# Softmax sums in attention: the 1e-9 added on VectorE, without GpSimd's two small additions

## The chip, the cores and the metric

The kernel runs on one core of a Trainium2 chip. The metric is device time in microseconds (us) of one execution. PE is TensorE, PEld its weight loads, DVE VectorE, ACT ScalarE, POOL GpSimd and SP the engine that issues the DMAs.

## The reference, cut to what matters

Block-causal attention over 8 batches of 8 heads (576 positions, 64 wide, blocks of 64), then a feed-forward layer whose activation is a rational function.

```python
scores = scale * np.matmul(q, k.transpose(0, 1, 3, 2))
scores = np.where(mask, scores, -1000000000.0)
scores = scores - np.max(scores, axis=-1, keepdims=True)
attn = np.exp(scores)
attn = attn / (np.sum(attn, axis=-1, keepdims=True) + 1e-09)
attn_out = np.matmul(attn, v)
# x: attn_out as 4608 tokens of 512
h = x @ w_in                                   # 2048 wide
P = a[0] + a[1] * h + a[2] * h**2 + a[3] * h**3
Q = 1.0 + np.abs(b[0]) * np.abs(h) + np.abs(b[1]) * h**2
out = (P / (Q + 1e-6)) @ w_out
```

## The kernel before, in words

**Attention** works on 32 visits, each a pair of heads of one batch. A visit has five query tiles t = 0 to 4 of 64, 128, 128, 128 and 128 rows, with 64, 192, 320, 448 and 576 keys, and both heads j = 0, 1 of a tile: ten items per visit, 320 in all. `load` fetches q, k and v on SP's queue; `prep` transposes q and k on PE and splits each into a high and a low part; three DMAs place the parts into kq. For each item `scores` multiplies into PSUM (L432, L433, mask in L436), and DVE takes the negative row maximum into nm (L437). For t = 4 the row of 576 keys lies in two PSUM banks, so there are two maxima, joined in L440.

One item later `expo` runs. ACT takes the exponential (L449) into the tile pt and writes each row's sum to sm: sm[:, j, 0], and for t = 4 a second part in sm[:, j, 1]. After the second head of a tile the group of both heads is normalised. For t = 4 POOL adds the two parts of sm (L455). POOL adds 1e-9 into the small tile rc (L456), DVE takes its reciprocal in place (L457), and POOL multiplies the probabilities by it: the first 64 keys into pk (L458), the rest in place (L462, once per head, t > 0 only). That is one group per query tile: 160 groups, 32 of them with t = 4. Nine items after the group's second head, `transp` transposes the probabilities on PE (L481) and splits them (ACT L486, DVE L487), and `pv` multiplies them by v (L500). The tiles rc, nm and sm have four buffers each; a pt of each size has one, and pk has two.

**The feed-forward layer** runs in two phases over the hidden width. The first takes 1280 of the 2048 hidden columns, in units that are emitted between the attention steps as soon as a batch's tokens are there; the second follows attention. A unit is a first product on PE (L207), the rational function on ACT, POOL and DVE (L214 to L219, L224 to L232), a split of g into gh on ACT (L239) and gl on POOL (L240), and the second product on PE (L257), which needs gl and gh.

**The weights** come as float64 bit patterns and are taken apart into two float32 parts by `place` (L129 to L149, on ACT, POOL and DVE). Of its 32 steps four are emitted by step 36 of attention, sixteen from step 44 to 59 and twelve from step 80 to 230.

**The order of work** on each engine is set when the program is built: the loops emit in the order of `attn_steps` and `Ffn.steps`, and the framework then settles the order of the instructions of each engine and places the waits. Each engine works its own list strictly in order.

The lines that matter here are L437, L440, L449, L455 to L462, L481, L240 and L257.

Of the kernel before, what the change touches and what calls it, by code (L numbers as in the profile page):

```python
# [14 lines left out]
ALU = mybir.AluOpType  # L15
# [46 lines left out]
def attn_ffn_kernel(  # L62
# [11 lines left out]
    nc = tc.nc  # L74
# [234 lines left out]
    with ExitStack() as actx:  # L309
# [101 lines left out]
        def pieces(t):  # L411
            return [(0, NK[t])] if t < 4 else [(0, 288), (288, 288)]
# [30 lines left out]
        def expo(p, t, j):  # L443
            s = st_[p]
            nq, n = NQ[t], NK[t]
            pt, pk, nm, sm = s[t]
            banks = s.pop((t, j))
            for i, (c0, w) in enumerate(pieces(t)):
                nc.scalar.activation(out=pt[:nq, j, c0:c0 + w], in_=banks[i][:nq, :w], func=AF.Exp,  # L449
                                     bias=nm[:nq, j, 0:1], scale=1.0, accum_out=sm[:nq, j, i:i + 1])  # L450
            if j == 0:
                return
            rc = att.tile([128, 2], F32, name=f"rc{p}_{t}", tag="rc", bufs=4)
            if t == 4:
                nc.gpsimd.tensor_tensor(out=sm[:, :, 0], in0=sm[:, :, 0], in1=sm[:, :, 1], op=ALU.add)  # L455
            nc.gpsimd.tensor_scalar_add(rc[:nq], sm[:nq, :, 0], 1e-9)  # L456
            nc.vector.reciprocal(rc[:nq], rc[:nq])  # L457
            nc.gpsimd.tensor_tensor(out=pk[:nq], in0=pt[:nq, :, 0:64],  # L458
                                    in1=rc[:nq].unsqueeze(2).to_broadcast([nq, 2, 64]), op=ALU.mult)
            if t > 0:  # L460
                for jj in range(2):
                    nc.gpsimd.tensor_scalar(out=pt[:nq, jj, 64:n], in0=pt[:nq, jj, 64:n],  # L462
                                            scalar1=rc[:nq, jj:jj + 1], scalar2=1.0,
                                            op0=ALU.mult, op1=ALU.mult)
# [48 lines left out]
        def attn_steps():  # L513
# [8 lines left out]
            for k in range(len(items) + ALAG2 + ALAG3 + 8):  # L522
                for x in [x for x in todo if x[0] == k]:
                    todo.remove(x)
                    x[1](*x[2])
                if k < len(items):
                    p, t, j = items[k]
                    ts = visits[p][1]
                    if (t, j) == (ts[0], 0):
                        if p + 1 < NV:  # L530
                            o0, o1, o2 = OFFS[len(ts)]
                            at(k + o0, load, p + 1)
                            at(k + o1, prep, p + 1, 0)
                            at(k + o2, prep, p + 1, 1)
                    at(k + ALAG2, expo, p, t, j)
                    if j == 1:
                        lag = min(ALAG3, nxt[k] - 1)
                        at(k + lag, transp, p, t)
                        if t in (2, 4):
                            at(k + lag + 1, pv, p, t // 4)  # L540
                            if t == ts[-1] and p + 1 < NV:
                                at(k + lag + 1, vprep, p + 1)
                    scores(p, t, j)
                yield k
# [87 lines left out]
```

## Time and profile before

| | |
|---|---|
| median of 3 runs | 1382.86 us (1381.88 to 1384.8) |
| the profiled execution | 1380.84 us |
| its span, first to last instruction | 1379.1 us |
| busy share: PE, PEld, DVE, ACT, POOL | 93%, 83%, 74%, 66%, 69% |
| instructions: DVE, POOL | 2048, 1240 |
| mean granted TensorE clock | 0.974 of full speed |

The busy share is an average over the span. The span has stretches of different kinds: attention starts up while weights are taken apart (to about 175 us), attention and the first phase of the feed-forward layer run side by side (to about 970 us), then the second phase runs alone.

### The profile page before, as it was taken

The page shows a single profiled execution, that of the slowest core. Times are in us where ns is not written, and L with a number is a line of the kernel's source. Part 1 is how long each engine was busy: PE and PEld are TensorE (multiplying, and loading weights), DVE is VectorE, ACT ScalarE, POOL GpSimd, SP SyncE. Part 2 cuts the span into 40 slices and gives each one's busy share as a digit, 9 for nine tenths or more (in the row PEclk, how much of TensorE's full clock was granted, in tenths as well). Part 3 has the DMA queues.
Part 4 walks back from the last instruction along what each step waited for, and adds up shares of the span by engine and source line. Part 5 has one row for each costly group of instructions (what it writes and reads, how often), then busy time and mean ns, then how long its engine had stood idle before and what let it go on. Part 6 is the DMA issues. An engine that isn't in the chain of part 4 may idle for free.

```text
span 1379.1 us, 24416 instructions
## 1 busy us (share of the span) xinstructions
PE 1278.1 (93%) x8088; PEld 1149.6 (83%) x8088; DVE 1027.2 (74%) x2048; ACT 909.4 (66%) x2250; POOL 958.2 (69%) x1240
## 2 busy tenths in 40 slices
PE   4677899999899979999999999999989999999997
PEld 3667788999888879888998999998979888888885
DVE  5898877787778857887767777776676767676675
ACT  4766767777677756777767777776645655555553
POOL 4889987687678747777767676666556666666654
PEclk9788999999999999999999999999999999999999
DMA  9778556666556655665654555652632233333332
GB/s 216 198 196 238 146 150 166 168 166 181 148 145 150 164 151 132 165 166 153 157 140 123 154 134 122 160 127 65 213 141 77 77 123 123 122 123 123 122 113 86
DMA packets 216925, 200.84 MB, mean 146 GB/s; under 512 B 129504, under 2 KB 184800, under 8 KB 216800
## 3 DMA queue, kind: packets, MB, share of 16 engines
q1 hardware_dynamic: 216736, 199.28, 53.6%
q8 instruction: 65, 1.06, 0.3%
q14 instruction: 60, 0.49, 0.1%
q0 software_dynamic: 64, 0.00, 0.0%
HBM read 98.57 MB, written 44.04 MB: 103 GB/s over the span
## 4 chain that ended last, share of the span: by engine, by line
PE 69%; DVE 9%; POOL 9%; DMA 5%; ACT 3%; issue 3%; SPq 1%; POOLq 0%; DVEq 0%; ACTq 0%
PE h L207 25%; PE o L257 24%; PE o L500 8%; PE t L481 4%; PE s L432 3%; PE s L433 2%; PE tp L366 2%; POOL gl L240 1%; POOL p L462 1%; DMA x<-xscr 1%; POOL u L217 1%; DVE v L231 1%; DVE nm L437 1%; POOL v L216 1%; DMA xscr<-x 1%
## 5 line engine op out<-in xcount | busy, mean ns | idle before, releaser
L207 PE MATMUL h<-x,wih 128*128 128x256 f32 (+1 forms) x1872 | 415.7, 313 | 9.0 <-DMA x<-xscr 7.9
L207 PEld LDWEIGHTS h<-x,wih 128*128 128x128 f32 x1872 | 309.7, 191 | 29.1 <-issue 6.6
L207 PE MATMUL h<-x,wil 128*128 128x256 f32 (+1 forms) x936 | 290.7, 311 | 0.0
L240 POOL TENSOR_TENSOR gl<-s,gh 128x512 fp32r<-128x512 f32 x144 | 188.8, 1313 | 106.4 <-ACT gh L239 103.0
L257 PE MATMUL o<-woh,gl 128*128 128x512 f32 x576 | 232.2, 403 | 12.1 <-POOL gl L240 10.6
L257 PE MATMUL o<-wol,gh 128*128 128x512 f32 x576 | 227.7, 396 | 0.0
L257 PE MATMUL o<-woh,gh 128*128 128x512 f32 x576 | 227.7, 395 | 0.0
L437 DVE TENSOR_REDUCE nm<-s 128x1 f32<-128x288 f32 (+4 forms) x384 | 161.7, 427 | 78.4 <-PE s L436 45.2
L449 ACT ACTIVATE p<-s,nm 128x288 f32<-128x288 f32 (+4 forms) x384 | 184.9, 485 | 48.3 <-DVE nm L437 35.0
L217 POOL TENSOR_TENSOR u<-v,u 128x512 f32<-128x512 f32 x144 | 189.6, 1317 | 9.8
L216 POOL TENSOR_SCALAR v<-u,bab 128x512 f32<-128x512 f32 x144 | 118.9, 826 | 98.1 <-ACT u L214 94.6
L207 PEld LDWEIGHTS h<-x,wil 128*128 128x128 f32 x936 | 178.7, 191 | 8.7
L462 POOL TENSOR_SCALAR p<-p,rc 128x128 f32<-128x128 f32 (+3 forms) x256 | 164.8, 655 | 29.6 <-DVE rc L457 27.7
L218 DVE TENSOR_TENSOR s<-s,h 128x512 f32<-128x512 f32 x144 | 98.5, 684 | 100.1 <-ACT s L215 99.4
L432 PE MATMUL s<-kq 128*128 128x256 f32 (+3 forms) x384 | 137.3, 360 | 24.3 <-DMA kq<-hl 8.9
L224 ACT ACTIVATE v<-u,qcb 128x512 f32<-128x512 f32 x144 | 104.6, 726 | 69.6 <-POOL u L217 68.9
L214 ACT ACTIVATE u<-h 128x512 f32<-128x512 f32 x144 | 85.9, 596 | 94.2 <-PE h L207 90.1
L239 ACT CAST gh<-s 128x512 fp32r<-128x512 f32 x144 | 89.2, 623 | 82.1 <-DVE s L232 81.5
L257 PEld LDWEIGHTS o<-woh,gl 128*128 128x128 f32 x576 | 109.2, 190 | 35.5 <-POOL gl L240 14.3
L257 PEld LDWEIGHTS o<-wol,gh 128*128 128x128 f32 x576 | 109.1, 189 | 22.2
L257 PEld LDWEIGHTS o<-woh,gh 128*128 128x128 f32 x576 | 109.3, 190 | 18.9
L433 PE MATMUL s<-kq 128*128 128x256 f32 (+3 forms) x384 | 120.1, 315 | 0.0
(105 smaller groups left out, 3043.5 us busy)
## 6 DMA issues: line engine op xcount, KB each, us to landing
kq<-hl SPq DMA_DIRECT2D x64, 432.0 KB, 4.3
kq<-hl SPq DMA_DIRECT2D x64, 288.0 KB, 5.3
x<-xscr SPq DMA_DIRECT2D x56, 256.0 KB, 4.2
xscr<-x SPq DMA_DIRECT2D x32, 320.0 KB, 4.7
qr<-in_q_dram SPq DMA_DIRECT2D x64, 144.0 KB, 2.9
kr<-in_k_dram SPq DMA_DIRECT2D x64, 144.0 KB, 3.0
kq<-hl SPq DMA_DIRECT2D x64, 144.0 KB, 4.8
pscr<-os SPq DMA_DIRECT2D x18, 512.0 KB, 2.9
```

The source lines that it names most:

```text
L207: nc.tensor.matmul(h[:, j, :], lhsT=w[:, dc, fs], rhs=xs[dc][:, hl, :], start=(dc == 0 and i == 0), stop=(dc == 3 and i == 2))
L216: nc.gpsimd.tensor_scalar(out=vt, in0=ut, scalar1=b1, scalar2=b0, op0=ALU.mult, op1=ALU.add)
L217: nc.gpsimd.tensor_tensor(out=ut, in0=vt, in1=ut, op=ALU.mult)
L224: nc.scalar.activation(out=vt, in_=ut, func=AF.Ln, bias=qcb)
L240: nc.gpsimd.tensor_tensor(out=gl.rearrange("p j t -> p (j t)"), in0=st, in1=gh.rearrange("p j t -> p (j t)").bitcast(F32), op=ALU.subtract)
L257: nc.tensor.matmul(self.o[m], lhsT=g[:, j, ms], rhs=w[:, f, :], start=(u == 0 and j == 0 and i == 0), stop=(u == nu - 1 and j == NBU[ph] - ...
L432: nc.tensor.matmul(ps[:, :ww], lhsT=kq[:, 0, qs], rhs=kq[:, 1, c0:c0 + ww], start=True, stop=False)
L433: nc.tensor.matmul(ps[:, :ww], lhsT=kq[:, 0, qs], rhs=kq[:, 2, c0:c0 + ww], start=False, stop=not last)
L437: nc.vector.reduce_max(out=nm[:nq, j, i:i + 1], in_=ps[:nq, :w], axis=AX.X, negate=True)
L449: nc.scalar.activation(out=pt[:nq, j, c0:c0 + w], in_=banks[i][:nq, :w], func=AF.Exp, bias=nm[:nq, j, 0:1], scale=1.0, accum_out=sm[:nq, j ...
L462: nc.gpsimd.tensor_scalar(out=pt[:nq, jj, 64:n], in0=pt[:nq, jj, 64:n], scalar1=rc[:nq, jj:jj + 1], scalar2=1.0, op0=ALU.mult, op1=ALU.mult)
L500: nc.tensor.matmul(o[:, s0:w], lhsT=vblock(vv, x), rhs=pp, start=(x == 0 and i == 0), stop=(x == nb - 1 and i == 2))
```

## The change

For every tile but t = 4, the addition of 1e-9 goes from POOL to DVE, with the same operands. For t = 4 one DVE instruction with two tensor inputs takes the place of POOL's two: it forms (sm[:, :, 0] + 1e-9) + sm[:, :, 1] into rc. The reciprocal behind it on DVE and the multiplications on POOL stay as they are.

```diff
             rc = att.tile([128, 2], F32, name=f"rc{p}_{t}", tag="rc", bufs=4)
             if t == 4:
-                nc.gpsimd.tensor_tensor(out=sm[:, :, 0], in0=sm[:, :, 0], in1=sm[:, :, 1], op=ALU.add)
-            nc.gpsimd.tensor_scalar_add(rc[:nq], sm[:nq, :, 0], 1e-9)
+                nc.vector.scalar_tensor_tensor(out=rc, in0=sm[:, :, 0], scalar=1e-9, in1=sm[:, :, 1],
+                                               op0=ALU.add, op1=ALU.add)
+            else:
+                nc.vector.tensor_scalar_add(rc[:nq], sm[:nq, :, 0], 1e-9)
             nc.vector.reciprocal(rc[:nq], rc[:nq])
```

## Rows read from the trace of the kernel before

**Rows 1.** The page's chain that ended last, by engine.

```profile
PE 69%; DVE 9%; POOL 9%; DMA 5%; ACT 3%; issue 3%; SPq 1%; POOLq 0%; DVEq 0%; ACTq 0%
```

**Rows 2.** Stretches: us; busy (instructions) PE, PEld, DVE, ACT, POOL; PEclk, DMA, GB/s.

```profile
35.00:110.00 75.00, 55.01 (x322) 49.42 (x321) 64.22 (x154) 52.46 (x158) 66.49 (x89) 0.79 0.77 200
110.00:175.00 65.00, 50.76 (x328) 46.54 (x329) 58.67 (x126) 46.77 (x135) 58.92 (x75) 0.87 0.69 183
175.00:970.00 795.00, 764.41 (x5462) 709.87 (x5461) 606.02 (x1322) 568.79 (x1545) 574.44 (x839) 1.00 0.58 147
```

**Rows 3.** That chain by line, 35 to 110, then 110 to 175 us.

```profile
by line: DMA sti<-in_moe_w_in_dram 14.1%; DMA sto<-in_moe_w_out_dram 12.0%; DVE nm L437 8.9%; DMA x<-xscr 6.7%; DVE pt2l L487 5.4%; DVE wpo L138 5.2%; issue 5.1%; DVE hl L371 4.6%; DVE wbo L134 4.4%; DVE wpo L139 4.2%; DVE wao L132 2.5%; PE
...
by line: POOL p L462 12.7%; issue 11.2%; POOL vpl L394 8.4%; DMA x<-xscr 7.7%; POOL wol L145 5.4%; POOL wai L130 4.6%; PE o L500 4.5%; POOL pk L458 4.2%; POOL wao L130 4.1%; POOL wil L145 3.8%; DVE wbo L134 3.3%; POOL rc L456 3.2%; DVE v L2
```

**Rows 4.** Pieces of that chain, 110 to 175 us: start, us, what.

```profile
140.14 0.60 POOL sm L455
...
171.75 0.16 POOL sm L455
```

**Rows 5.** Busy us (instructions) of L456 in the same three stretches.

```profile
35.00:110.00 75.00, 5.24 (x15) 0.79 0.77 200
110.00:175.00 65.00, 3.88 (x11) 0.87 0.69 183
175.00:970.00 795.00, 34.16 (x130) 1.00 0.58 147
```

**Rows 6.** Groups by line and form: busy us, mean ns, idle before.

```profile
L217 POOL TENSOR_TENSOR u<-v,u 128x512 f32<-128x512 f32 x144 | 189.6, 1317 | 9.8
L456 POOL TENSOR_SCALAR rc<-sm 128x2 f32<-128x2 f32 x128 | 35.8, 280 | 40.5 <-ACT p L449 32.0
L455 POOL TENSOR_TENSOR sm<-sm 128x2 f32<-128x2 f32 x32 | 7.9, 246 | 13.5 <-ACT p L449 13.5
...
L440 DVE TENSOR_TENSOR nm<-nm 128x1 f32<-128x1 f32 x64 | 22.1, 345 | 0.5
```

**Rows 7.** Single lines: duration ns min/median/max, first and last start us.

```profile
L457 DVE RECIPROCAL rc<-rc x160: 145/158/168, 23.7 to 965.1; 128x2 f32<-128x2 f32 x128, 64x2 f32<-64x2 f32 x32
...
L231 DVE SCALAR_TENSOR_TENSOR v<-u,v x90: 661/692/2055, 148.3 to 1071.7; 128x512 f32<-128x512 f32 x90
```

**Rows 8.** Waits over the whole span: us in total, times, longest us.

```profile
POOL pk L458 <- PE t L481: 42.8, 33, 4.3
POOL rc L456 <- ACT p L449: 35.6, 35, 3.2
...
DVE rc L457 <- POOL rc L456: 33.6, 45, 1.8
```

**Rows 9.** Waits of PE, then of its weight loads, 175 to 970 us.

```profile
PE o L500 <- DVE pt0l L487: 6.0, 4, 2.1
PE o L257 <- POOL gl L240: 4.9, 6, 1.4
...
PEld o L257 <- POOL gl L240: 7.0, 9, 1.6
```

**Rows 10.** Timeline of one t = 3 group: start us, us, engine, line.

```profile
499.89 0.24 ACT L449 ACTIVATION_READ_ACCUMULATOR p<-s,nm 128x1 f32 x1
...
500.22 0.22 POOL L456 TENSOR_SCALAR rc<-sm 128x2 f32<-128x2 f32 x1 [1.37 <-ACT p L449]
500.47 0.17 DVE L457 RECIPROCAL rc<-rc 128x2 f32<-128x2 f32 x1
...
500.74 0.58 POOL L462 TENSOR_SCALAR p<-p,rc 128x384 f32<-128x384 f32 x1 [0.29 <-DVE rc L457]
```

**Rows 11.** Timeline of PE: start us, us, engine, line.

```profile
546.00 0.40 PE L257 MATMUL o<-woh,gh 128*128 128x512 f32 x1
...
546.47 0.27 PE L481 MATMUL t<-ident,pk 128*128 128x128 f32 x1
...
546.72 0.48 PE L257 MATMUL o<-wol,gh 128*128 128x512 f32 x1
```

## The prediction

> **What bounds the kernel now.** I first read the chain that ended last [rows 1]: PE holds 69% of it, DVE and POOL 9% each. So PE bounds most of the span, and each of the two engines that the change touches decides something somewhere. To find where, I cut the span into stretches [rows 2]; subtract a busy time from its stretch to get the idle time. From 35 to 110 us PE idles 20.0 of 75 us, from 110 to 175 us 14.2 of 65, from 175 to 970 us only 30.6 of 795. After 970 us none of the touched lines runs (L457's last start is 965.1 us [rows 7]), so that part stays.
>
> The chain by line tells who decides in the two early stretches [rows 3]. From 35 to 110 us it is DMAs that bring weights, and DVE: the seven DVE lines that the row shows before it is cut hold 35.2%, 26.4 us. From 110 to 175 us it is POOL: eight lines, 46.4%, 30.2 us, and the moved L456 is one of them with 3.2%, 2.1 us. The same change therefore loads the engine that decides in one stretch and relieves the one that decides in the next. From 175 us on, PE is 96% busy, and what can be won there is limited to its 30.6 us of idle time.
>
> **Removed from POOL.** 160 additions of 1e-9 and 32 of two partial sums, with means of 0.26 to 0.28 and 0.25 us [rows 5, 6]: about 160 x 0.276 + 32 x 0.25 = 52 us of POOL work. Its worth by stretch:
>
> From 110 to 175 us, 11 groups. On the chain lie 2.1 us of L456 [rows 3] and 0.60 + 0.16 us of L455 [rows 4], 2.9 us together. All of L456's work there is 3.88 us [rows 5], with about two groups of t = 4 at 0.25 us 4.4 us. The gain lies between 2.9 and 4.4 us; I take 3.7, the middle, as POOL is 91% busy there [rows 2] and most of what stands in front of a later instruction delays it.
>
> From 175 to 970 us, PE waits for POOL's gl 4.9 us, and its weight loads 7.0 us, in 15 waits [rows 9]. Each can start earlier by what a group in front of it on POOL saves: 34.16 us / 130 = 0.26 [rows 5], and one fifth of 0.25, 0.31 us. 15 x 0.31 is 4.7 us. A product and its weight load often wait for the same gl, so I take half: a gain of 2.3 us, with 0 and 5 as ends.
>
> From 35 to 110 us POOL's lines hardly stand in the chain: 5.24 us [rows 5] at no gain.
>
> **Added to DVE.** 160 additions, one per group, since the t = 4 form does both sums at once. The trace of before has no addition of this size on DVE. The nearest below is the reciprocal of the same tile, one input, 0.16 us and never above 0.168 [rows 7]. The nearest above is L440, also tiny but with two inputs in SBUF like the t = 4 form: 0.345 us on average [rows 6]. I take 0.35 for the 32 t = 4 forms, 0.23 for the 128 others, between the two, and so 0.25 us a group; the ends are 0.16 and 0.35.
>
> From 35 to 110 us, 15 groups [rows 5] cost 15 x 0.25 = 3.8 us of DVE time. DVE's chain share against its busy time is 26.4 / 64.2 = 0.41, from a row that is cut off, so I count half: a loss of 1.9 us. Ends: 15 x 0.16 x 0.5 = 1.2 and, all on the path, 15 x 0.35 = 5.3.
>
> From 175 to 970 us, 130 groups add 32.5 us. Against that, DVE today stands 33.6 us, 45 times, before L457 waiting for POOL [rows 8]. That stall was itself a wait for ACT's sum plus POOL's addition; the second part, 0.25 us each time, goes: 11 us. What DVE gains in load is 21 us on 189 us of idle time [rows 2]. PE's wait for DVE's pt0l, 6.0 us [rows 9], grows in the ratio 189 / 168, by 0.8 us. Ends: 0 and 2.
>
> **Moved waits.** POOL's wait for ACT's sums (35.6 us for L456 [rows 8]) goes to DVE's new addition, with reduce_max and the rest of DVE's list queued behind it. DVE waited at that place for the later event already, so this costs nothing new. POOL now waits at L458 or L462 for DVE alone. The group at 500 us shows the handover [rows 10]: ACT ends at 500.13, POOL's addition ends at 500.44, the reciprocal starts at 500.47, POOL's product at 500.74. An addition on DVE saves one of three handovers and costs about what POOL's did, so one group is hardly shorter; it is POOL's time that is saved. A new wait is that DVE must not write rc before POOL has read the buffer of four groups earlier. 160 groups in 941 us are 5.9 us apart, four of them 23.5 us, while the longest wait before L458 is 4.3 us [rows 7, 8]: nothing, unless POOL falls behind by 20 us. No DMA and no instruction of SP's queue moves.
>
> **The sum.** -3.7 + 1.9 - 2.3 + 0.8 = -3.3 us, from 1380.84 to 1377.5 us for the profiled execution. That execution lies 2.0 us below the median of the runs, so I forecast 1382.86 - 3.3 = 1379.6 us. By the ends it is between -8.2 (-4.4 + 1.2 - 5) and +4.4 (-2.9 + 5.3 + 2): 1374.7 to 1387.3 us. A measurement of this kernel can tell about 0.2%, 2.8 us, from no change, so the forecast lies just beyond that bound.
>
> **Rivals.** *A bigger gain.* DVE no longer depends on a POOL that is itself held up (42.8 us before L458, waiting for PE [rows 8]), and POOL's backlog from 110 to 175 us dissolves: half of PE's 14.2 us of idle time there and all 11.9 us of waits for gl go, 1364 us. For it: 52 us of work leave POOL. Against: PE's other waits are for DMA, ACT and DVE, and DVE gets fuller.
>
> *Nothing.* The relief between 110 and 175 us is eaten up by the load before it, and later PE's own work covers all: 1381 to 1385 us. PE's 96% from 175 us on speaks for it.
>
> *Slower, by collision of DVE with POOL.* In this trace a DVE instruction with its inputs in SBUF is sometimes very long: L231's fastest is 0.661 us, its longest 2.055 us [rows 7], and L440, one element wide, averages 0.345. If the additions wait out whatever POOL is doing, such as a 1.3 us product [rows 6], the price is 0.16 us plus POOL's busy share (89% early, 72% later [rows 2]) times half of 1.3: 0.74 and 0.63 us. Then the early stretch loses half to all of 15 x 0.74, 5.6 to 11.1 us; later DVE gains 130 x 0.63 - 11 = 71 us, and PE's 6.0 us of waits grow by 189 / 118, by 3.6 us. With POOL's 6.0 us off, this is +3.2 to +8.7, 1386 to 1392 us. It decides from about 0.5 us per addition (7.5 x 0.5 + 6.0 x (189 / 135 - 1) = 6.2). Against it, the reciprocal in this same place never exceeded 0.168 us, and the group's next POOL instruction waits for this very addition, so POOL is often idle then. The Trainium skill, "SBUF — State Buffer", section "Who interferes with whom", speaks against the change here: VectorE and GpSimd share a port pair, taken exclusively for a whole instruction, by a VectorE instruction with two SBUF inputs or in a two-port mode. L231 and L440 agree with that; no row shows that a plain addition of two elements would be caught too.
>
> *Slower or faster, by another order.* The lists are not in the order in which the code emits: three products of one block of L257 have attention's L481 between them [rows 11]. Taking 192 instructions from one list and putting 160 into another can shift what stands next to what everywhere. If a quarter of PE's 34.2 idle us before 175 us is lost or won by it, the time is 8.6 us off: 1391 or 1374 us.
>
> **How the numbers follow.** Small gain 0.40, of which 0.24 beyond the bound of 0.2% and 0.16 within it (its own range is 1376 to 1383 us); bigger gain 0.13; nothing 0.13; collision 0.15; another order 0.14 against and 0.05 for. Faster: 0.24 + 0.13 + 0.05 = 0.42. Same: 0.16 + 0.13 = 0.29. Slower: 0.29. The range reaches from near the bigger gain to the far end of the slower cases: 1366 to 1392 us.
>
> **What would show it.** Right: DVE's new additions average 0.2 to 0.3 us; L457 no longer waits for POOL; POOL's busy time falls by about 50 us; PE's idle time falls from 110 to 175 us and grows a little before. Wrong: additions above 0.5 us; PE waiting longer for pt0l or other DVE results than it saves on gl; or a PE list in another order, with new waits far from these lines.

## The result and the profile after

| | before | after |
|---|---|---|
| median | 1382.47 us (1381.43 to 1386.36, 7 runs) | 1389.44 us (1386.69 to 1393.72, 7 runs) |
| the profiled execution's span | 1379.1 us | 1387.6 us |

The changed kernel is **slower**: the ratio is 1.0046, 95% interval 1.0032 to 1.0059, which is 6.4 us (4.4 to 8.2). The forecast was 1379.6 us, 3.3 us faster. The time lies inside the range that was given, but on the wrong side of no change.

The busy times of the kernel before, whose span is 1379.1 us:

```profile
PE 1278.1 (93%) x8088; PEld 1149.6 (83%) x8088; DVE 1027.2 (74%) x2048; ACT 909.4 (66%) x2250; POOL 958.2 (69%) x1240
```

The page of the changed kernel: its span, the busy times, and the chain by engine.

```profile
span 1387.6 us, 24515 instructions
...
PE 1282.5 (92%) x8088; PEld 1153.3 (83%) x8088; DVE 1056.5 (76%) x2208; ACT 909.0 (66%) x2250; POOL 896.0 (65%) x1048
...
PE 66%; DVE 12%; DMA 9%; POOL 5%; ACT 4%; issue 3%; SPq 1%; POOLq 0%; DVEq 0%; ACTq 0%
```

The answer to [rows 1] is that DVE's share of the chain rose from 9 to 12% and POOL's fell from 9 to 5%. DMA's rose from 5 to 9%, which no part of the prediction had spoken of. POOL's busy time fell by 62 us and DVE's rose by 29 us. PE idles 105.1 us (span less busy time), against 101.0 before. So of the 8.5 us that the span is longer, 4.1 are idle time of PE, and 4.4 are busy time for the same 8088 products, at a mean granted clock of 0.972 against 0.974.

The three stretches, with the columns of [rows 2]:

```profile
35.00:110.00 75.00, 53.12 (x327) 47.75 (x327) 67.90 (x172) 53.80 (x160) 59.33 (x70) 0.83 0.78 204
110.00:175.00 65.00, 50.03 (x308) 46.20 (x309) 55.74 (x125) 43.47 (x123) 48.54 (x57) 0.82 0.68 178
175.00:970.00 795.00, 759.40 (x5381) 704.51 (x5379) 620.24 (x1444) 562.70 (x1536) 521.71 (x675) 0.99 0.59 147
```

PE's idle time is 21.9, 15.0 and 35.6 us, against 20.0, 14.2 and 30.6. It was forecast to fall from 110 to 175 us, where POOL was the bound; POOL's busy time did fall there by 10.4 us, and PE idles as long as before.

The new additions on DVE, by line and form (busy us, mean ns, idle time before), with L440 for comparison:

```profile
L458 DVE TENSOR_SCALAR rc<-sm 128x2 f32<-128x2 f32 x96 | 26.9, 280 | 6.3 <-ACT p L449 5.7
...
L440 DVE TENSOR_TENSOR nm<-nm 128x1 f32<-128x1 f32 x64 | 22.3, 349 | 0.6
...
L458 DVE TENSOR_SCALAR rc<-sm 64x2 f32<-64x2 f32 x32 | 11.6, 362 | 0.4 <-ACT p L449 0.4
...
L455 DVE SCALAR_TENSOR_TENSOR rc<-sm 128x2 f32<-128x2 f32 x32 | 8.6, 270 | 14.0 <-ACT p L449 14.0
```

Their price is (26.9 + 11.6 + 8.6) / 160 = 0.29 us each, a little under L440's 0.35. Single instructions (min/median/max) of L458:

```profile
L458 DVE TENSOR_SCALAR rc<-sm x128: 139/169/1191, 22.9 to 963.8; 128x2 f32<-128x2 f32 x96, 64x2 f32<-64x2 f32 x32
```

The same for the reciprocal, which stands in L459 now:

```profile
L459 DVE RECIPROCAL rc<-rc x160: 144/156/168, 23.2 to 972.4; 128x2 f32<-128x2 f32 x128, 64x2 f32<-64x2 f32 x32
```

The waits that moved, over the whole span (us in total, times, longest), answer to [rows 8]:

```profile
POOL p L464 <- DVE rc L459: 70.3, 49, 3.4
...
POOL pk L460 <- PE t L483: 65.0, 42, 6.9
...
DVE rc L455 <- ACT p L449: 14.0, 16, 1.5
...
DVE rc L458 <- ACT p L449: 6.0, 14, 1.0
```

The two additions wait 20 us for ACT, less than the 33.6 us that the reciprocal stood waiting for POOL. POOL's in-place products waited 27.7 us for rc before; now it is 70.3, as that wait contains the one for ACT. Its wait for PE before pk, 42.8 us in [rows 8], is 65.0.

Where PE's waiting went is seen in its own list. First before, then after, DMA's lines and gl's:

```profile
PE o L257 <- POOL gl L240: 10.6, 9, 4.0
PE s L432 <- DMA kq<-hl: 8.9, 3, 4.7
PE h L207 <- DMA x<-xscr: 7.9, 3, 3.0
...
PE tp L366 <- DMA qr<-in_q_dram: 5.6, 2, 4.2
...
PE tp L366 <- DMA kr<-in_k_dram: 4.3, 4, 1.5
```

```profile
PE s L432 <- DMA kq<-hl: 22.4, 9, 5.2
PE h L207 <- DMA x<-xscr: 7.3, 6, 3.6
...
PE tp L366 <- DMA kr<-in_k_dram: 4.5, 5, 1.7
PE tp L366 <- DMA qr<-in_q_dram: 4.3, 1, 4.3
...
PE s L432 <- DMA x<-xscr: 3.0, 1, 3.0
...
PE o L257 <- POOL gl L240: 2.7, 3, 1.6
```

gl costs PE 2.7 us instead of 10.6. That looks like the relief of POOL that was forecast, and it isn't: the two kernels of the next section have the change's work in the lists of before (first line) and the work of before in the new lists (second line), and the short wait comes with the lists.

```profile
PE o L257 <- POOL gl L240: 9.8, 7, 4.7
...
PE o L257 <- POOL gl L240: 2.6, 4, 0.9
```

PE waits 41.5 us for DMAs (kq, x, qr and kr) instead of 26.7. No DMA was added, removed or resized. What did change is the order: when the instructions of both programs are matched one to one, 6323 of PE's 8088 places hold another instruction than before, and so do 442 of the 794 places of SP, which issues the DMAs.

### The profile page after: what moved, and what is told of

Same layout as the page of the kernel before. It is cut to its first block, busy times and chain, and to the rows that moved or that the text cites. A ratio compares the mean times of both kernels' runs of the same rounds, so it can differ in the third digit from the quotient of the medians.

```text
span 1387.6 us, 24515 instructions
## 1 busy us (share of the span) xinstructions
PE 1282.5 (92%) x8088; PEld 1153.3 (83%) x8088; DVE 1056.5 (76%) x2208; ACT 909.0 (66%) x2250; POOL 896.0 (65%) x1048
## 4 chain that ended last, share of the span: by engine, by line
PE 66%; DVE 12%; DMA 9%; POOL 5%; ACT 4%; issue 3%; SPq 1%; POOLq 0%; DVEq 0%; ACTq 0%
PE h L207 24%; PE o L257 22%; PE o L502 8%; PE t L483 4%; DMA kq<-hl 3%; PE s L432 3%; PE s L433 2%; DMA x<-xscr 2%; PE tp L366 1%; DMA xscr<-x 1%; DVE nm L437 1%; DMA kr<-in_k_dram 1%; DVE s L232 1%; POOL u L217 1%; DVE u L230 1%
## 5 line engine op out<-in xcount | busy, mean ns | idle before, releaser
L207 PE MATMUL h<-x,wih 128*128 128x256 f32 (+1 forms) x1872 | 422.7, 317 | 10.5 <-DMA x<-xscr 7.3
L207 PEld LDWEIGHTS h<-x,wih 128*128 128x128 f32 x1872 | 314.4, 194 | 34.1 <-issue 5.5
L464 POOL TENSOR_SCALAR p<-p,rc 128x128 f32<-128x128 f32 (+3 forms) x256 | 158.9, 632 | 76.7 <-DVE rc L459 70.3
L216 POOL TENSOR_SCALAR v<-u,bab 128x512 f32<-128x512 f32 x144 | 122.4, 850 | 121.7 <-ACT u L214 106.0
L207 PEld LDWEIGHTS h<-x,wil 128*128 128x128 f32 x936 | 181.7, 194 | 8.6
L432 PE MATMUL s<-kq 128*128 128x256 f32 (+3 forms) x384 | 137.8, 362 | 41.0 <-DMA kq<-hl 22.4
L224 ACT ACTIVATE v<-u,qcb 128x512 f32<-128x512 f32 x144 | 104.6, 726 | 70.6 <-POOL u L217 70.3
L483 PE MATMUL t<-ident,p 128*128 128x128 f32 (+1 forms) x672 | 114.0, 279 | 7.3 <-DVE x L506 2.7
```

Source lines behind the costliest of these rows:

```text
L207: nc.tensor.matmul(h[:, j, :], lhsT=w[:, dc, fs], rhs=xs[dc][:, hl, :], start=(dc == 0 and i == 0), stop=(dc == 3 and i == 2))
L216: nc.gpsimd.tensor_scalar(out=vt, in0=ut, scalar1=b1, scalar2=b0, op0=ALU.mult, op1=ALU.add)
L224: nc.scalar.activation(out=vt, in_=ut, func=AF.Ln, bias=qcb)
L432: nc.tensor.matmul(ps[:, :ww], lhsT=kq[:, 0, qs], rhs=kq[:, 1, c0:c0 + ww], start=True, stop=False)
L483: nc.tensor.transpose(ps[:, i, :nq], src, ident[:nq, :nq])
```

## The experiments

Two theories stood at the start. **Load**: 160 additions on DVE hold up PE. **Order**: the framework settles the lists anew, and the new lists are worse. All ratios below are to the kernel before on the same chip in the same job, with 95% intervals.

### The new work in the old order, and the old work in the new order

A function behind the kernel reads a table of the emitted instructions' places and ties each engine's list to that order. The ties are meant to fix the sequence and to make no instruction wait for another's end. In the traces, all 8088 instructions of PE come in the sequence of the kernel whose order is held. What the ties cost by themselves was not measured with the kernel before held to its own order; in another order they cost little (0.9906 as the framework made it, 0.9915 and 0.9918 held, further down).

```diff
     with _tile.TileContext(nc, schedule_with_timeline_sim=True) as tc:
         attn_ffn_kernel(tc, *args)
+        _hold_order(tc)
...
+def _hold_order(tc):
...
+            k += int(s)
+            if prev is not None:
+                tc.add_manual_dep(mine[engine][k], prev.name,
+                                  mybir.DependencyInfo(mybir.DependencyClass.NoSync, mybir.DependencyReason.DATA),
+                                  reason="order")
+            prev = mine[engine][k]
```

The first kernel has the change's work and the lists of before; each new addition stands directly ahead of its reciprocal.

> All of the change's work (160 additions on DVE, 192 gone from POOL), but each engine's list held in the order of the kernel before, each new addition directly ahead of its reciprocal. Theory order (the slowdown is the reshuffled order, the moved work itself is worth the forecast -3.3 us): 1379 us, at most 1383. Theory load (160 additions on DVE hold up PE, whatever the order): 1387 to 1391, as the changed kernel.

Measured: 1386.37 us, ratio 1.0019 (1.0000 to 1.0038). That is +2.6 us (0 to 5.3), between both expectations: the moved work isn't the gain that was forecast, and it isn't the whole loss either. Its page:

```profile
span 1385.0 us, 24478 instructions
...
PE 1287.4 (93%) x8088; PEld 1159.5 (84%) x8088; DVE 1057.2 (76%) x2208; ACT 910.3 (66%) x2250; POOL 901.2 (65%) x1048
```

PE's idle time is 97.6 us here, 3.4 less than before's 101.0, which is what the forecast's sum said. By stretch (the columns of [rows 2]) the signs come as forecast too:

```profile
35.00:110.00 75.00, 54.69 (x303) 48.15 (x304) 67.99 (x166) 51.12 (x155) 58.28 (x69) 0.75 0.74 192
110.00:175.00 65.00, 52.42 (x332) 48.20 (x332) 57.37 (x132) 45.56 (x130) 52.68 (x60) 0.85 0.74 193
175.00:970.00 795.00, 766.43 (x5451) 712.84 (x5449) 632.92 (x1458) 570.22 (x1552) 532.41 (x685) 0.99 0.58 147
```

That is 20.3, 12.6 and 28.6 us of idle time, against 20.0, 14.2 and 30.6. But PE is busy 9.3 us longer for the same 8088 products: the mean granted clock was 0.967 in this execution and 0.974 in the profiled one of before, whose other executions lie between 0.965 and 0.974. The profile of before is thus one of its executions at the highest clock, and what PE idles in it at its usual clock of 0.969 to 0.971 is not on record. The two profiles alone would have confirmed a wrong sum; the medians decide.

The second kernel has the sums on POOL and the changed kernel's lists. POOL's sums stand where the additions on DVE stood in the overall order.

> The work of the kernel before (all small sums on POOL), each engine's list held in the order of the changed kernel. Theory order: slow like the changed kernel or a little worse, 1389 to 1394 us. Theory load: as the kernel before, 1381 to 1385 us.

Measured: 1411.94 us, ratio 1.0224 (1.0198 to 1.0250). Its page:

```profile
span 1408.1 us, 24439 instructions
...
PE 1295.6 (92%) x8088; PEld 1163.2 (83%) x8088; DVE 1016.6 (72%) x2048; ACT 908.7 (65%) x2250; POOL 951.6 (68%) x1240
...
PE 59%; DVE 12%; POOL 11%; DMA 8%; ACT 5%; issue 3%; SPq 1%; POOLq 0%; DVEq 0%; ACTq 0%
```

That is above what either theory named. Load alone can't explain it: with all of that load taken off DVE, the new order is slower still, by 1.0224 against 1.0046. But the places of POOL's sums in these lists were chosen here and not by the framework, so how much of this is the order and how much those places is open. More than half of the extra time is PE's busy time: it is 17.5 us longer than before's, at a mean granted clock of 0.961, and PE's idle time is 11.5 us longer (112.5).

### How far a tiny move stirs the order

The change was then made for a few groups alone, with the lists left to the framework. The condition is that of the very first group here; it is `p == 5`, `p == 4` or `p == 8` for the five groups of one visit.

```diff
+            if p == 0 and t == 0:
+                if t == 4:
...
+                else:
+                    nc.vector.tensor_scalar_add(rc[:nq], sm[:nq, :, 0], 1e-9)
+            else:
...
+                nc.gpsimd.tensor_scalar_add(rc[:nq], sm[:nq, :, 0], 1e-9)
```

> The change for the very first group alone (p = 0, t = 0), the other 159 as before, orders left to the framework, which then sets 5810 of 8088 of PE's places otherwise. Theory order: any time from 1374 to 1392 us, off 1382.5 by more than 2.8 us though only one addition of some 0.2 us moved. Theory load: 1382.5 us, within 1 us of the kernel before.

Measured: 1384.57 us, ratio 1.0023 (1.0008 to 1.0037). One addition of 160 moved, and by the ratio the time is 3.2 us longer, with the interval clear of no change (the medians alone differ by 2.0). It is above what load allows, by little, and beyond the 2.8 us of the order theory only by the ratio. Its granted clock is lower too (0.967 in the median of its runs, 0.969 in those of before), and its PE idles 98.7 us in the profile, no more than before's.

> The change for the five groups of the sixth visit (p = 5) alone, orders left to the framework (5553 of PE's places differ). Theory order: any time from 1374 to 1392 us, and another than with one group. Theory load: 1382.5 us, within 1 us of the kernel before.

Measured: 1368.22 us, ratio 0.9906 (0.9884 to 0.9928). Five additions moved, and the kernel is 13 us faster than before, beyond the fast end that the order theory named:

```profile
span 1364.1 us, 24397 instructions
...
PE 1279.4 (94%) x8088; PEld 1152.3 (84%) x8088; DVE 1028.3 (75%) x2053; ACT 909.1 (67%) x2250; POOL 952.0 (70%) x1234
```

PE's busy time is that of before within 1.3 us; its idle time is 84.7 us instead of 101.0. That can't be five additions of 0.3 us. Another visit:

> The change for the five groups of the fifth visit (p = 4) alone, order left to the framework (5700 of PE's places differ from before). Theory order: another draw, 1366 to 1392 us, not tied to the moved work. If moving a visit's sums to DVE early is itself good: near the sixth visit's 1368 us.

Measured: 1378.32 us, ratio 0.9956 (0.9938 to 0.9973): a third time, and not that of the sixth visit.

### Is every order a draw?

The reverse: the change for all groups but those of one visit (`p != 2`, `p != 5`, `p != 8` in the same condition).

> The change for all groups but the five of the third visit (p = 2), order left to the framework (6064 of PE's places differ from the changed kernel, 5947 from before). Theory order: another draw for nearly the same work, 1372 to 1395 us, off the changed kernel's 1389.4 us by 2.8 us or more. Theory load: 1388 to 1391 us, as the changed kernel.

Measured: 1389.66 us, ratio 1.0038 (1.0025 to 1.0051): the time of the changed kernel, though 6064 of PE's places differ from it. Order had expected another time; this one is a miss. It raised the question of whether the framework's orders with the sums on DVE are slow as a kind ("level") or whether each is a draw of its own ("draw"). Three more orders were taken for it.

> The change for all groups but the five of the sixth visit (p = 5), order left to the framework (5985 of PE's places differ from the changed kernel). Theory draw (each order is a draw, whatever the work): anywhere from 1366 to 1392 us. Theory level (with the sums on DVE the framework's orders are all slow): 1387 to 1392 us, like the two such orders measured.

Measured: 1395.75 us, ratio 1.0080 (1.0059 to 1.0100).

> The change for all groups but the five of the ninth visit (p = 8), order left to the framework (5219 of PE's places differ from the changed kernel). Theory draw: anywhere from 1366 to 1392 us. Theory level: 1387 to 1392 us.

Measured: 1402.12 us, ratio 1.0129 (1.0105 to 1.0153). Both lie above the 1392 us to which either theory went, and on the slow side that "level" named.

> The change for the five groups of the ninth visit (p = 8) alone, order left to the framework (4775 of PE's places differ from before). Theory draw: anywhere from 1366 to 1392 us. Theory level (orders made with the sums on POOL are faster): 1368 to 1385 us, as the four such orders measured.

Measured: 1386.43 us, ratio 1.0015 (1.0003 to 1.0027), 1.4 us above the span that "level" named. By its ratio it lies between the kernel before and the one with a single group on DVE (1.0023), and below all the framework's orders with the sums on DVE. PE's longest waits for DMA in the slowest of the four, all but the ninth visit:

```profile
PE s L432 <- DMA kq<-hl: 18.7, 8, 5.3
...
PE h L207 <- DMA x<-xscr: 11.0, 5, 6.5
```

Set beside each other, with PE's waits for all DMAs added up from its list of waits:

| sums on | order | ratio | PE waits for DMA, us |
|---|---|---|---|
| POOL | before | 1 | 26.7 |
| POOL but one group | its own | 1.0023 | 28.9 |
| POOL but one visit (sixth, fifth, ninth) | their own | 0.9906, 0.9956, 1.0015 | 18.1, 22.0, 26.1 |
| DVE (the change) | its own | 1.0046 | 41.5 |
| DVE but one visit (third, sixth, ninth) | their own | 1.0038, 1.0080, 1.0129 | 34.5, 33.9, 41.4 |
| POOL | the changed kernel's | 1.0224 | 35.6 |
| DVE | before's | 1.0019 | 27.2 |
| DVE | that of the sixth visit alone | 0.9918 | 23.3 |
| POOL | that of the sixth visit alone | 0.9915 | 19.4 |

The four orders that the framework makes with nearly all sums on DVE are all slower than the five it makes with nearly all on POOL; the ratios of the two sets don't overlap, though the nearest intervals do (1.0008 to 1.0037 and 1.0025 to 1.0051). Part of the distance is the work: it costs 1.0019 in the order of before, and with that taken off, the DVE orders lie at 1.0019 to 1.0110, beside the slowest of the others. So it isn't shown that orders made for DVE are worse as a kind. Within each set the order is a draw of about 1%.

PE's wait for DMAs goes mostly with the order: 33.9 to 41.5 us in the orders made for DVE, whichever engine does the sums in them, and 18.1 to 28.9 us in those made for POOL. Each figure is of one execution, and the same order can give 26.7 to 32.0 us (that of before, with the two kernels of the next section, which have 32.0 and 27.8). This wait alone does not set the time: the work of before in the new order waits less for DMAs than the changed kernel and is far slower, and the kernel with 32.0 us is faster than before.

The other part is PE's busy time. In the slowest of the four, at a granted clock of 0.961:

```profile
span 1395.8 us, 24498 instructions
...
PE 1289.2 (92%) x8088; PEld 1161.7 (83%) x8088; DVE 1051.3 (75%) x2203; ACT 911.5 (65%) x2250; POOL 902.6 (65%) x1054
```

Against the profile of before, PE is busy 11.1 us longer and idles 5.6 us longer. The granted clock goes with the order as well: in the median of the runs it is 0.962 here and 0.969 for before in the same job, while in the faster order of the sixth visit it is 0.971 to 0.974. Why the clock is lower in the slow orders was not tried.

### The price of each half, in the order of before

> The order of the kernel before, with POOL's 160 additions of 1e-9 left out and nothing added on DVE (the reciprocal reads the sum itself; for t = 4 POOL still adds the two parts). It prices POOL's relief alone. By the prediction's terms (-3.7 and -2.3 us, plus DVE's shorter stalls): 1375 to 1379 us. If POOL's relief is worth nothing in this order: 1381 to 1385 us.

```diff
             if t == 4:
                 nc.gpsimd.tensor_tensor(out=sm[:, :, 0], in0=sm[:, :, 0], in1=sm[:, :, 1], op=ALU.add)
-            nc.gpsimd.tensor_scalar_add(rc[:nq], sm[:nq, :, 0], 1e-9)
-            nc.vector.reciprocal(rc[:nq], rc[:nq])
+            nc.vector.reciprocal(rc[:nq], sm[:nq, :, 0])
```

Measured: 1378.32 us, ratio 0.9965 (0.9952 to 0.9978), -4.8 us (-6.6 to -3.0), as the prediction's terms had it. It is not POOL's relief alone: the reciprocal also has one instruction less ahead of it in each group.

```profile
span 1378.5 us, 24319 instructions
...
PE 1281.3 (93%) x8088; PEld 1153.8 (84%) x8088; DVE 1013.0 (73%) x2048; ACT 909.9 (66%) x2250; POOL 908.2 (66%) x1080
```

In the stretch from 175 to 970 us the weight loads' wait for gl, 7.0 us in [rows 9], is now:

```profile
PEld o L257 <- POOL gl L240: 4.7, 7, 1.3
```

> The order of the kernel before, POOL's small sums all kept, and DVE makes the same additions as well, into a spare part of the tile, each directly ahead of its reciprocal. It prices DVE's 160 additions alone. By the prediction's terms (+1.9 and about +1.5 us): 1384 to 1387 us. If DVE's load is what made the same work 3.8 us slower in this order: 1387 to 1391 us.

```diff
+            rx = att.tile([128, 6], F32, name=f"rc{p}_{t}", tag="rc", bufs=4)
+            rc, rs, rd = rx[:, 0:2], rx[:, 2:4], rx[:, 4:6]
...
+                nc.vector.scalar_tensor_tensor(out=rd, in0=sm[:, :, 0], scalar=1e-9, in1=sm[:, :, 1],
+                                               op0=ALU.add, op1=ALU.add)
...
+                nc.vector.tensor_scalar_add(rd[:nq], sm[:nq, :, 0], 1e-9)
             nc.vector.reciprocal(rc[:nq], rc[:nq])
```

For t = 4 POOL's sum of the two parts goes to rs, so that DVE still finds both in sm. Measured: 1387.76 us, ratio 1.0029 (1.0017 to 1.0041), +4.0 us (2.4 to 5.7). The median lies in the range of the load theory; as before measured 1383.6 us in this job, 1.1 more than in the first, the two theories are hardly told apart. The extra additions by form:

```profile
L462 DVE TENSOR_SCALAR rc<-sm 128x2 f32<-128x2 f32 x96 | 25.6, 266 | 2.9 <-ACT p L449 2.5
...
L462 DVE TENSOR_SCALAR rc<-sm 64x2 f32<-64x2 f32 x32 | 12.3, 383 | 0.0
...
L458 DVE SCALAR_TENSOR_TENSOR rc<-sm 128x2 f32<-128x2 f32 x32 | 6.2, 193 | 6.6 <-ACT p L449 6.6
```

They cost 44.1 / 160 = 0.28 us each, close to the 0.29 of the changed kernel. The two halves together make -0.8 us, and both at once had measured +2.6 (0 to 5.3); the intervals overlap. In an unchanged order the change is a few us at most, and not the gain that was forecast.

### The faster order

The lists of the kernel with the sixth visit's sums on DVE, held for other work.

> All of the change's work (every small sum on DVE), each list held in the order that the run with the sixth visit alone had (1368.2 us). If the order sets the time and the moved work is worth a few us either way: 1365 to 1374 us, faster than both kernels; by the +3.8 us that the same work cost in the order of the kernel before, 1372. If 160 additions on DVE cost what the changed kernel lost: 1375 us or more.

Measured: 1371.94 us, ratio 0.9918 (0.9903 to 0.9933), as the order theory had it. The same work had 1.0046 in its own order.

> The work of the kernel before, all small sums on POOL, in that same order. Five groups of 160 go back to POOL. Theory order: 1366 to 1371 us. If the five moved groups themselves had brought the 14 us: 1380 to 1384 us.

Measured: 1371.36 us, ratio 0.9915 (0.9900 to 0.9930). The order brings the gain, not the five groups; and between the work of before and that of the change there is nothing to tell in it.

> The order that the run with the sixth visit alone had, POOL's 160 additions of 1e-9 left out and nothing added on DVE. If the price of the sums and the order are separate things: the 4.8 us of POOL's relief off the 1371.4 us of the work before in this order, 1365 to 1369 us, the fastest of all. If the relief is worth something only in the order made for the work before: 1370 to 1374 us.

Measured: 1362.39 us, ratio 0.9849 (0.9830 to 0.9868), the fastest of all.

```profile
span 1358.8 us, 24299 instructions
...
PE 1275.2 (94%) x8088; PEld 1150.0 (85%) x8088; DVE 1016.7 (75%) x2048; ACT 909.3 (67%) x2250; POOL 909.0 (67%) x1080
```

That is below the range of either reading. The order brings 0.85% and POOL's missing additions 0.66% more, where they brought 0.35% in the order of before; the intervals of both, from different jobs, are too wide to call this a difference. PE's idle time is 83.6 us. This kernel leaves out the 1e-9, as the expectation says. Of the kernels that add it, the one with the sixth visit alone is the fastest, 1368.2 us.

## Why the prediction was wrong, step by step

**What bounds the kernel.** In the order of before that reading held: both halves of the change have their effect with the sign that the stretches gave. In the changed kernel's order POOL was relieved from 110 to 175 us and PE's idle time did not fall (15.0 against 14.2 us).

**Removed from POOL.** -3.7 - 2.3 = -6.0 us was forecast; POOL's 160 additions alone brought -4.8 (-6.6 to -3.0), with t = 4's sums still there and a shorter way to the reciprocal. Within its interval this step was right. (The means of 0.26 to 0.28 us hold from 175 us on; by the prediction's own rows L456 takes 5.24 / 15 = 0.35 before.)

**Added to DVE.** The mean of 0.25 us was near the 0.29 measured, but made up otherwise: the plain additions cost 38.5 / 128 = 0.30 instead of 0.23, the two-input form 0.27 instead of 0.35. In time, +1.9 + 0.8 = +2.7 us was forecast, with 11 us of DVE's old stall counted in its favour; the additions alone, without that credit, cost +4.0 (2.4 to 5.7). The forecast lies in that interval, near its low end.

**Moved waits.** DVE's additions wait 20 us where its reciprocal waited 33.6, so no new stall shows. That "no instruction of SP's queue moves" holds for the edit and not for the lists: 442 of SP's 794 places changed.

**The sum, the first step that failed,** came to -3.3 us, and the measured change is +6.4, so it missed by 9.7 us. It failed already in the order for which it was worked out: there the change measured +2.6 us (0 to 5.3), which leaves out -3.3, and 5.9 of the 9.7 us are lost here. Relief that was 1.2 us smaller than 6.0 and load that was 1.3 us larger than 2.7 make up 2.5 of them; the halves measured alone make -0.8. The other 3.4 us, between the halves and the whole, stay open; the intervals allow them to be noise. The forecast gain was the difference of two terms, 6.0 and 2.7 us, whose ends lay 12.6 us apart (-8.2 to +4.4); it was smaller than what was unknown about it.

**The second step that failed** is one that the sum takes for granted: that the lists stay as they are. It makes up the other 3.8 us or so. The prediction saw in [rows 11] that the lists are not in the order of emission, put "another order" down as a rival with 0.14 for the slow side and 0.05 for the fast one, and named a PE list in another order among the signs of being wrong; that sign came. The runs show that the order is worth more than the change: the change's work takes 1.0019 in the order of before, 1.0046 in its own and 0.9918 in that of the sixth visit. A single addition moved stirs 5810 of PE's places. Of the changed kernel's 0.46%, about 0.19% is the work in the old order and the rest, 1.0046 / 1.0019 = 1.0027, the new order; the intervals of both runs touch, so the shares are rough.

**The collision rival.** Its price did not come: 0.29 us, not above 0.5. Its mechanism is there all the same. L458 has one input, runs 0.139 us at best and 1.191 at worst, and its mean is nearly twice its median of 0.169. The trace of the changed kernel tells which additions are long. Of the 160, 74 start while POOL is idle, and all of these take 0.141 to 0.172 us. The other 86 start while a POOL instruction runs and average 0.41 us; 52 of them take 0.25 us or more, and 48 of the 52 end within 0.04 us after a POOL instruction has ended. The longest, from DVE's timeline, with POOL's product beside it from POOL's (start us, us):

```profile
824.52 1.30 POOL L217 TENSOR_TENSOR u<-v,u 128x512 f32<-128x512 f32 x1
...
824.65 1.19 DVE L458 TENSOR_SCALAR rc<-sm 64x2 f32<-64x2 f32 x1
```

So most long additions last until the POOL instruction beside them has ended, as the rival had it, and the mean stays low because nearly half of all find POOL idle. The trace of before showed the same in L440: 9 of its 64 start with POOL idle and take 0.141 to 0.159 us, the other 55 average 0.38. The Trainium skill, "SBUF — State Buffer", section "Who interferes with whom", names `tensor_scalar` among the instructions that can take the port pair shared with GpSimd; the long additions agree with that, which the prediction had left open. That the port is what they wait for was not tried by itself.

**What stays open.** What in an order makes it slow is not settled, neither PE's longer waits for kq and x nor its lower granted clock. Both were found with the order and not changed alone; SP's list, for one, was not exchanged by itself.

## What to carry to other kernels

Where a framework settles the lists, an edit's price is the work in an unchanged order plus a draw of a new order; here the draw was worth up to 1%, more than either half of the edit. Hold the order to measure an edit, compare medians and not two profiles, and draw several orders to look for a faster one. And a forecast that is the difference of two terms of 3 to 6 us is a forecast of no change.

## What had not been expected of the hardware

An addition of two elements per partition on DVE took 0.139 to 1.191 us, the long ones mostly until POOL's instruction beside them had ended, and a reciprocal of the same tile never more than 0.168, in the same lists and next to each other, though 76 of the 160 start beside a running POOL instruction. (With both additions kept, one reciprocal of 160 took 0.367.) And two executions at granted clocks of 0.974 and 0.967 differ by 9.3 us of PE's busy time for the same products in the same order, more than the whole effect under study.
